# First k load on the ScalarE queue, contiguous turned rows, table transposes moved, and a new instruction plan, in a fused convolution and FFN kernel

## The chip, the cores and the metric

The kernel runs on one core of a Trainium2 chip. The metric is device time in microseconds (us) of one execution, the median of several runs. TensorE (PE in the profile) does the matmuls and transposes, VectorE (DVE) and ScalarE (ACT) the elementwise work and the copies out of PSUM, GpSimd (POOL) a few small operations, and SyncE (SP) issues most transfers. [...]

## The reference, cut to what matters

Two layers, each a gated long convolution (A) and a gated feed-forward network (B), on x of 2048 rows by 512 channels:

```python
def _A_ref(q, k, v, shift_k, ssm_k, ssm_D):
    k_shift = sum over t of k_pad[:, t:t+S, :] * shift_k[:, ks-1-t]     # 4 taps
    kv = k_shift * v
    y = irfft(rfft(kv padded to 2S) * rfft(ssm_k padded to 2S))[:S]     # long convolution over the rows
    return q * (y + kv * ssm_D)

def _B_ref(x, w_gate, w_up, w_down):                                    # D = 512, F = 1792
    return (silu(x @ w_gate) * (x @ w_up)) @ w_down

x = A_q
for layer in (0, 1):
    x = x + _A_ref(layernorm(x), A_k, A_v, A_shift_k, A_ssm_k, A_ssm_D)
    x = x + _B_ref(layernorm(x), B_w_gate, B_w_up, B_w_down)
```

(The loop and the sum over t are written out in the original; padding is shortened here.) The convolution result y does not depend on x or the layer, so it is computed once and used in both layers.

## The kernel before

The rows are cut into four blocks of 512, each held as 128 partitions by R = 4 rows. The long convolution is done block by block with cosine and sine tables ("fwd", and "inv", their transposes): each block of kv and of ssm_k (h) is turned into a spectrum by matmuls ("ps<-vt,fwd", "ps<-hs,fwd"), spectra are multiplied on VectorE ("t", "Z"), and matmuls with "inv" give y. The shift by taps is a matmul, too: four matmuls per 128 channels with diagonal matrices "dg" that hold the taps.

A planner in the kernel's own Python puts every operation into a list with an engine, an assumed cost and the buffers it reads and writes, and then fixes each engine's order by those costs. Where it foresees that TensorE is idle, it fills in matmuls on the identity ("wm"), whose results nobody reads:

```python
    def issue(self, seq, place, when, warm_until, warm):
        ...
                if start < warm_until and start - t > 0.5:
                    for ring, i in [(r, i) for r in ("pf", "pd", "pc") for i in range(self.rings[r])]:
                        if busy.get((ring, i), 0.0) <= t:
                            n = int((start - t - 0.4) / 0.085)
                            if n > 0:
                                warm(ring, i, n)
                            break
```

PSUM has eight buffers in three rings: "pf" (4), "pc" (2) and "pd" (2). The start of the program, for the first block:

```python
    def load_k(b, due=None, after=()):
        if b == 0:
            kn[b] = new("s8", "kn", [P, R, D])
            add("SP", 0.55, lambda: nc.sync.dma_start(out=kn[b].t[:], in_=k_t[:, b]), w=[kn[b]], lat=4.0, due=due)
            return
        ...                                   # other blocks: a transposing transfer

    def transpose_k(b, ring, engs):           # block 0: turned on TensorE, copied out by ACT and DVE in turn
        kT[b] = new("k", "kTb", [P, KD, PADL + L], parts=KD + 1)
        ...
        for dt in range(KD):
            pt = new(ring, "pt", [P, R, P], BF16)
            ...                               # four transposes of kn into pt (L379)
            dst = lambda dt=dt: kT[b].t[:, dt, PADL:PADL + L].rearrange("d (p r) -> d r p", r=R)
            ...                               # copy pt to dst (L383 ACT, L385 DVE)

    def shift_mul(b, ring, conv, after=()):
        for r in range(R):
            ...                               # per dt, per tap j:
                       [(kT[b].t[:, dt, PADL + r - j:PADL + r - j + R * (P - 1) + 1:R], dg.t[:, dt, j, :])
                        for j in range(KS)]
            ...                               # block 0: DVE multiplies the result by vt (L502)

    ...
    add("PE", 0.25, turn_taps, r=[tapR, ident], w=[pt4])                   # L928
    add("DVE", 0.1, lambda: nc.vector.tensor_copy(out=tapT.t[:], ...))     # L930
    for dt in range(KD):
        add("DVE", 0.6, ... out=dg.t[:, dt], ident * tapT[:, dt] ...)      # L933, four diagonals each
    transpose_k(0, "pf", ("ACT", "DVE"))
    hs = transpose_h(0, "pf", (2, 0, 1, 3), False, ("ACT", "DVE"))         # L475, L479, L482
    ...
    shift_mul(0, "pf", False)
    ...                                                                    # statistics, spectrum of h
    for n in range(2):
        it = new("pf", "it", [P, NI, P])
        ...                                   # seven transposes of fwd (L953), copied to inv by ACT (L955)
    X[0] = spectrum("X0")
    direct(vt[0], X[0], "pf", ("ACT", "ACT"))                              # spectrum of kv, block 0
    for slot in (0, 2, 1, 3):
        product(0, 0, [slot], False)                                       # L620, L624
```

The FFN of one unit (a layer, a block, and half of its rows) takes gate and up matmuls into "pf" (zT is the normalised x, turned), Silu and a copy on ScalarE (L837, L841), their product on VectorE (L844), and down matmuls into "pd" (L851). The result is added to x by VectorE (L870), or, in units that X_PE names, x is fed into the same PSUM sum by one more matmul (L817) for each 128 rows. Other switches choose engines unit by unit: ST1 and ST2 compute the sums of the layernorm on ScalarE, N_ACT and Z_ACT apply it there.

Of the kernel before, what the change touches and what calls it, by code (L numbers as in the profile page):

```python
# [9 lines left out]
P = 128  # L10
# [3 lines left out]
ACT = mybir.ActivationFunctionType  # L14
# [2 lines left out]
LN_EPS = 1e-5  # L17

NB = 4
SLK = 8.52  # L20
H_DMA = lambda b: b in {2, 3}
ST1 = lambda l, c, h: (l, c, h) in {(0, 1, 1), (0, 2, 0), (0, 3, 0), (1, 0, 1)}
ST2 = lambda l, c, h: (l, c, h) in {(0, 1, 1), (0, 3, 1), (1, 0, 0)}
ASL = 8.04
K_ACT = lambda b: b in {3}
PASSES = 1
PW = 1.2
PD_ACT, KV_ACT, ST_ACT = True, True, False
HSL = 13.4
Z_ACT = lambda l, c, h: (l, c, h) in {(0, 3, 1), (1, 1, 0), (1, 1, 1)}  # L30
N_ACT = lambda l, c, h: (l, c, h) in {(0, 2, 0), (0, 2, 1), (1, 2, 1), (1, 3, 0), (1, 3, 1)}
Z_DMA = lambda i, j: False
D_DMA = lambda l, c, h: False
X_PE = lambda l, c, h: (l, c, h) in {(0, 3, 1), (1, 1, 0), (1, 2, 0), (1, 3, 1)}
RINGS = {}
T0, FLOOR = 37.71, 9.21
DUR = [20.73, 19.38, 17.95, 16.46, 26.14, 17.1, 26.09, 16.75, 22.3, 20.61, 21.16, 19.35, 17.53, 22.2, 16.85, 27.0]
STRETCH = {1: {"PE": 2.88, "DVE": 1.23, "ACT": 4.33, "POOL": 1.0, "SP": 160.46},
           2: {"PE": 3.08, "DVE": 1.77, "ACT": 1.75, "POOL": 1.0, "SP": 1.07},
           3: {"PE": 3.04, "DVE": 1.08, "ACT": 2.72, "POOL": 1.0, "SP": 1.04}}  # L40
R = 4


# [23 lines left out]
class Plan:  # L67
# [1 line left out]

    LOOSE = ("pc", "ks")  # L70
    WAIT = {"PE": 0.1, "DVE": 0.15, "ACT": 0.1, "POOL": 0.1, "SP": 0.1}
    SAME = {"PE": 0.0, "DVE": 0.06, "ACT": 0.05, "POOL": 0.1, "SP": 0.0}
    CROSS = {"PE": 0.3, "DVE": 0.2, "ACT": 0.25, "POOL": 0.15, "SP": 0.0}

    def __init__(self, rings):
# [196 lines left out]
def kernel(  # L272
# [14 lines left out]
    nc = tc.nc  # L287
# [26 lines left out]
    def new(ring, name, shape, dtype=BF16, parts=1):  # L314
        space = psp if ring in ("pf", "pc", "pd") else pool

        def make(slot):
            tag = f"{ring}{slot}" if ring != "one" else name
            return space.tile(list(shape), dtype, name=name, tag=tag)
        return plan.buf(ring, name, make, parts)  # L320
# [35 lines left out]
    def load_h(b, eng="SP", due=None, after=()):  # L356
        hn[b] = new("s8" if b == 1 else "h", "hn", [P, KD, L], parts=1)
        q = nc.sync if eng == "SP" else nc.scalar
        return add(eng, 0.55, lambda: q.dma_start(out=hn[b].t[:], in_=h3[:, :, b * L:(b + 1) * L]), w=[hn[b]], lat=(5.0, 10.0)[b] if b < 2 else 6.0, due=due, after=after)

    def load_k(b, due=None, after=()):
        if b == 0:
            kn[b] = new("s8", "kn", [P, R, D])
            add("SP", 0.55, lambda: nc.sync.dma_start(out=kn[b].t[:], in_=k_t[:, b]), w=[kn[b]], lat=4.0, due=due)
            return
        kT[b] = new("s8" if b == 1 else "k", "kTb", [P, KD, PADL + L])
        add("SP", 2.2, lambda: nc.sync.dma_start_transpose(out=kT[b].t[:], in_=k3[b * L - PADL:(b + 1) * L]),
            w=[kT[b]], lat=12.0 if b == 1 else 8.0, due=due, after=after)

    def transpose_k(b, ring, engs):  # L370

        kT[b] = new("k", "kTb", [P, KD, PADL + L], parts=KD + 1)
        add("POOL", 0.2, lambda: nc.gpsimd.memset(kT[b].t[:, :, 0:PADL], 0.0), w=[(kT[b], (KD,))])
        for dt in range(KD):
            pt = new(ring, "pt", [P, R, P], BF16)

            def go(pt=pt, dt=dt):
                for r in range(R):
                    nc.tensor.transpose(pt.t[:, r, :], kn[b].t[:, r, dt * P:(dt + 1) * P], ident.t[:])  # L379
            add("PE", pe(R, P), go, r=[kn[b], ident], w=[pt])  # L380
            dst = lambda dt=dt: kT[b].t[:, dt, PADL:PADL + L].rearrange("d (p r) -> d r p", r=R)
            if engs[dt % len(engs)] == "ACT":
                add("ACT", act(D), lambda pt=pt, dst=dst: nc.scalar.copy(out=dst(), in_=pt.t[:]), r=[pt], w=[(kT[b], (dt,))])  # L383
            else:
                add("DVE", tt1(D), lambda pt=pt, dst=dst: nc.vector.tensor_copy(out=dst(), in_=pt.t[:]), r=[pt],  # L385
                    w=[(kT[b], (dt,))])

    def load_v(b, due=None, after=()):
# [172 lines left out]
    def transpose_h_dma(b):  # L561
        hr = new("s8", "hr", [P, R, KD, P], parts=KD)
        hs = new("hs", "hs", [P, R, D], parts=R)
        for dt in range(KD):
            add("ACT", act(D), lambda dt=dt: nc.scalar.copy(
                out=hr.t[:, :, dt], in_=hn[b].t[:, dt, :].rearrange("d (p r) -> d r p", r=R)), r=[hn[b]], w=[(hr, (dt,))],
                conv=True)
        for r in range(R):
            turned[b] = add("SP", 1.25, lambda r=r: nc.sync.dma_start_transpose(
                out=hs.t[:, r].rearrange("p (k f) -> p k f", k=KD), in_=hr.t[:, r]), r=[hr], w=[(hs, (r,))], lat=3.0 if b == 1 else 1.4, conv=True)  # L570
        return hs

    def shift_mul_t(b):

        a, c = new("s8", "ka", [P, 2, R, KD, P], parts=2 * KD), new("s8", "kc", [P, 2, R, KD, P], parts=2 * KD)
        for j, (t, h) in ((3, (a, 0)), (2, (a, 1)), (1, (c, 0)), (0, (c, 1))):
            for dt in range(KD):
                add("ACT", 0.615, lambda j=j, t=t, h=h, dt=dt: nc.scalar.activation(
                    out=t.t[:, h, :, dt], in_=kT[b].t[:, dt, PADL - j:PADL - j + L].rearrange("d (p r) -> d r p", r=R),
                    func=ACT.Copy, scale=tapF.t[:, dt, j:j + 1]), r=[kT[b], tapF], w=[(t, (h * KD + dt,))], conv=True)  # L580
        for t, h in ((a, 1), (c, 0), (c, 1)):
            dve(4 * D, lambda t=t, h=h: nc.vector.tensor_add(out=a.t[:, 0], in0=a.t[:, 0], in1=t.t[:, h]),
                [(t, range(h * KD, h * KD + KD))], [(a, range(KD))], conv=True)
        ks = c
        for r in range(R):
            add("SP", 1.25, lambda r=r: nc.sync.dma_start_transpose(
                out=ks.t[:, 0, r], in_=a.t[:, 0, r]), r=[(a, range(KD))], w=[(c, (r,))], lat=4.0, conv=True)
        for h in range(2):
            sl = slice(2 * h, 2 * h + 2)
            dve(2 * D, lambda sl=sl: nc.vector.tensor_mul(  # L590
                out=vt[b].t[:, sl, :], in0=ks.t[:, 0, sl].rearrange("p r k d -> p r (k d)"), in1=vt[b].t[:, sl, :]),
                [(c, (2 * h, 2 * h + 1))], [(vt[b], (2 * h, 2 * h + 1))], conv=True)
# [214 lines left out]
    def ffn(unit):  # L807
# [78 lines left out]
                                             allow_small_or_imprecise_dtypes=True), w=[fq], due=-50)  # L886
    add("POOL", 0.6, lambda: make_identity(nc, ident.t[:]), w=[ident])
    add("ACT", 1.5, lambda: nc.scalar.activation(out=warm1.t[:], in_=nhalf.t[:], func=ACT.Silu), r=[nhalf], w=[warm1], due=-50)
    load_k(0, -60)
    tapR = new("dn", "tapR", [KD, P, KS])  # L890
    add("SP", 0.5, lambda: nc.sync.dma_start(out=tapR.t[:], in_=A_shift_k.rearrange("(dt p) j -> dt p j", p=P)), w=[tapR],
        lat=2.4, due=-70)
    load_h(0, "ACT", -59)
    ph = new("s8", "ph", [P, NS, P], I32, parts=2)
    load_v(0, -59)
# [32 lines left out]
            nc.tensor.transpose(pt4.t[:, j, :], tapR.t[:, :, j], ident.t[0:KD, 0:KD])  # L928
    add("PE", 0.25, turn_taps, r=[tapR, ident], w=[pt4])
    add("DVE", 0.1, lambda: nc.vector.tensor_copy(out=tapT.t[:], in_=pt4.t[:].rearrange("p j dt -> p dt j")), r=[pt4], w=[tapT])  # L930
    add("DVE", 0.1, lambda: nc.vector.tensor_copy(out=tapF.t[:], in_=tapT.t[:]), r=[tapT], w=[tapF])
    for dt in range(KD):
        add("DVE", 0.6, lambda dt=dt: nc.vector.tensor_tensor(  # L933
            out=dg.t[:, dt], in0=ident.t[:].rearrange("p (o f) -> p o f", o=1).to_broadcast((P, KS, P)),
            in1=tapT.t[:, dt, :].rearrange("p (j o) -> p j o", o=1).to_broadcast((P, KS, P)), op=ALU.mult),
            r=[ident, tapT], w=[(dg, (dt,))])
# [9 lines left out]
        half(hs, ev, par, 2.0 / N, "pf", ("ACT", "ACT"), False)  # L946
        butterfly(ev, G[0], par, False)
    for n in range(2):
        it = new("pf", "it", [P, NI, P])

        def go(it=it, n=n):
            for i in range(NI):
                nc.tensor.transpose(it.t[:, i, :], fwd.t[:, n * NI + i, :], ident.t[:])  # L953
        add("PE", pe(NI, P), go, r=[fwd, ident], w=[it])
        add("ACT", act(NI * P), lambda it=it, n=n: nc.scalar.copy(out=inv.t[:, n * NI:(n + 1) * NI, :], in_=it.t[:]),  # L955
            r=[it], w=[(inv, (n,))])
# [64 lines left out]

    with tc.manual_schedule(engines={mybir.EngineType.DVE, mybir.EngineType.Activation, mybir.EngineType.PE,
                                     mybir.EngineType.Pool, mybir.EngineType.SP}):
        plan.issue(*plan.order(PASSES), T0, warm)

# [1 line left out]
_INS = ['A_q', 'A_k', 'A_v', 'A_shift_k', 'A_ssm_k', 'A_ssm_D', 'B_x', 'B_w_gate', 'B_w_up', 'B_w_down']  # L1027
# [26 lines left out]
```

## Time and profile before

| | |
|---|---|
| time, median of 3 runs | 357.86 us (357.56 to 357.94) |
| span of the profiled execution | 356.5 us |
| TensorE busy | 347.6 us |
| VectorE busy | 281.1 us |
| ScalarE busy | 238.0 us |
| GpSimd busy | 39.3 us |
| first matmul of the FFN starts | 37.09 us |

Busy time of an engine is the time in which it has an instruction at work; matmuls are pipelined, so the duration of one (0.38 us for 512 columns) is longer than the distance from one to the next. A line of the timeline gives the start, the length, the engine, the source line, the operation, the tiles it writes and reads, and how many instructions are merged; in brackets stands how long the engine was idle before it and who ended that. A line of the waits gives the total, the number and the longest in us. A row of the DMA list ends with the median time from issue to landing in us.

### The profile page before, as it was taken

Reading aid. Unit: us, or ns where it says so; the run is one execution under the profiler, and the core shown is the slowest. Engines: PE = TensorE matmul, PEld = TensorE weight load, DVE = VectorE, ACT = ScalarE, POOL = GpSimd, SP = SyncE. Lnnn points to the kernel's source line nnn. Section 1 sums busy time; section 2 is a strip of 40 time slices with the busy share of each in tenths; the row PEclk is TensorE's granted clock in tenths of the full one; section 3 lists DMA queues with packets and bytes.
Section 4 is the critical chain, followed back from the end, with each engine's and each line's share of the span. In section 5 each row is a group of like instructions: output and inputs, shape, how many; then the busy total and the mean of one; then the engine's idle time right before and its main releaser. Section 6 shows DMA issues by size and latency. Waiting matters only on the chain.

```text
span 356.5 us, 6735 instructions
## 1 busy us (share of the span) xinstructions
PE 347.6 (97%) x2689; PEld 254.4 (71%) x2712; DVE 281.1 (79%) x517; ACT 238.0 (67%) x454; POOL 39.3 (11%) x42
## 2 busy tenths in 40 slices
PE   7999999999999999999999999999999999999996
PEld 6655985867778585868668685858686777768673
DVE  6997999999989999999999999889985323626020
ACT  4587693838878493648878994848484775647352
POOL 1010010130320200111121000201101000101000
PEclk9999999999999999999999999999999999999999
DMA  7999021010241341010311042010103020101000
GB/s 263 306 353 293 2 69 22 0 31 2 45 119 45 63 147 31 0 31 1 79 40 31 1 116 63 2 29 3 31 29 31 30 31 1 31 1 31 30 2 29
DMA packets 37897, 21.98 MB, mean 62 GB/s; under 512 B 29797, under 2 KB 35690, under 8 KB 37866
## 3 DMA queue, kind: packets, MB, share of 16 engines
q1 hardware_dynamic: 37336, 21.03, 22.9%
q10 hardware_dynamic: 530, 0.53, 0.5%
q8 instruction: 21, 0.34, 0.4%
q14 instruction: 10, 0.08, 0.1%
HBM read 12.33 MB, written 2.10 MB: 40 GB/s over the span
## 4 chain that ended last, share of the span: by engine, by line
PE 49%; DVE 35%; ACT 10%; POOL 3%; issue 2%; DMA 1%; ACTq 0%; POOLq 0%; DVEq 0%
PE pf L335 30%; PE pd L851 15%; DVE m L518 4%; DVE ht L844 3%; DVE bnst L706 3%; DVE t L641 3%; DVE t L635 3%; DVE t L651 2%; POOL rstd L736 2%; ACT H L423 2%; DVE Z L656 2%; PE ps L335 2%; PE wm L1020 1%; DVE t L620 1%; DVE Z L648 1%
## 5 line engine op out<-in xcount | busy, mean ns | idle before, releaser
L335 PE MATMUL pf<-zT,wu_sb 128*128 128x256 bf16 x896 | 116.1, 273 | 0.1
L335 PE MATMUL pf<-zT,wg_sb 128*128 128x256 bf16 x896 | 116.1, 273 | 0.0
L335 PEld LDWEIGHTS <-wg_sb 128*128 128x128 bf16 x896 | 87.6, 98 | 18.9 <-issue 0.8
L851 PE MATMUL pd<-wd_sb,ht 128*128 128x512 bf16 x434 | 98.6, 380 | 1.5 <-DVE ht L844 0.8
L335 PEld LDWEIGHTS <-wu_sb 128*128 128x128 bf16 x896 | 87.6, 98 | 11.1
L837 ACT ACTIVATE sg<-pf 128x512 bf16<-128x512 f32 x112 | 68.9, 615 | 18.2 <-PE pf L335 16.7
L851 PEld LDWEIGHTS <-ht 128*128 128x128 bf16 x448 | 43.6, 98 | 49.8 <-DVE ht L844 1.2
L841 ACT CAST ht<-pf 128x512 bf16<-128x512 f32 x112 | 67.3, 601 | 15.0 <-PE pf L335 14.6
L844 DVE TENSOR_TENSOR ht<-ht,sg 128x1024 bf16<-128x1024 bf16 x64 | 39.5, 619 | 25.7 <-ACT ht L841 25.7
L711 POOL TENSOR_TENSOR rstd<-ve,nhalf 128x2 f32<-128x2 f32 x25 | 26.0, 1039 | 203.2 <-DVE ve L709 180.8
L706 DVE BATCH_NORM_STATS2 bnst<-xc 128x6 f32<-128x512 bf16 x50 | 32.5, 685 | 6.2 <-ACT xc L857 5.6
L863 ACT CAST dn<-pd 128x512 bf16<-128x512 f32 x24 | 12.9, 591 | 34.5 <-PE pd L851 34.5
L870 DVE TENSOR_TENSOR xc<-xc,dn 128x1024 bf16<-128x1024 bf16 x12 | 8.2, 686 | 17.8 <-ACT dn L863 17.8
L635 DVE TENSOR_TENSOR t<-X,G 128x2048 bf16<-128x2048 bf16 x18 | 21.9, 1219 | 0.0
L641 DVE TENSOR_TENSOR t<-X,G 128x2048 bf16<-128x2048 bf16 x18 | 21.9, 1217 | 0.0
L736 POOL TENSOR_TENSOR rstd<-ve,nhalf 128x2 f32<-128x2 f32 x7 | 12.0, 1719 | 80.0 <-DVE ve L732 80.0
L423 ACT ACTIVATE X<-ps 128x512 bf16<-128x512 f32 x32 | 18.8, 635 | 1.2 <-PE ps L335 1.1
L423 ACT ACTIVATE H<-ps 128x512 bf16<-128x512 f32 x24 | 13.4, 645 | 4.3 <-PE ps L335 4.3
L656 DVE TENSOR_TENSOR Z<-Z,t 128x2048 bf16<-128x2048 bf16 x12 | 14.7, 1222 | 0.1
L651 DVE TENSOR_TENSOR t<-t,t 128x2048 bf16<-128x2048 bf16 x12 | 14.6, 1221 | 0.1
L335 PE MATMUL ps<-vt,fwd 128*128 128x512 bf16 x54 | 14.4, 380 | 0.1
L335 PEld LDWEIGHTS <-fwd 128*128 128x128 bf16 x96 | 9.3, 98 | 7.2
(95 smaller groups left out, 316.5 us busy)
## 6 DMA issues: line engine op xcount, KB each, us to landing
vt<-in_A_v_dram SPq DMA_DIRECT2D x4, 512.0 KB, 4.6
xc<-in_A_q_dram SPq DMA_DIRECT2D x4, 512.0 KB, 4.8
out_dram<-xc SPq DMA_DIRECT2D x16, 128.0 KB, 1.7
wg_sb<-in_B_w_gate_dram SPq DMA_DIRECT2D x1, 1792.0 KB, 9.2
wu_sb<-in_B_w_up_dram SPq DMA_DIRECT2D x1, 1792.0 KB
wd_sb<-in_B_w_down_dram SPq DMA_DIRECT2D x1, 1792.0 KB, 12.3
hn<-in_A_ssm_k_dram SPq DMA_DIRECT2D x3, 512.0 KB, 7.6
hn<-in_A_ssm_k_dram ACTq DMA_DIRECT2D x1, 512.0 KB, 3.9
```

The source lines that it names most:

```text
L335: nc.tensor.matmul(o, lhsT=lhsT, rhs=rhs, start=(n == 0), stop=(n == len(terms) - 1))
L423: add("ACT", act(D), lambda: nc.scalar.activation(out=view(), in_=ps.t[:], func=ACT.Copy, scale=scale), r=[ps], w=[(buf, keys)], conv=conv)
L635: dve(n * D, lambda t1=t1, part=part: nc.vector.tensor_mul(out=t1.t[:], in0=x.t[:, sl, 0, :], in1=g.t[:, sl, part, :]), [(x, key(slots, (0 ...
L641: dve(n * D, lambda t2=t2, part=part: nc.vector.tensor_mul(out=t2.t[:], in0=x.t[:, sl, 1, :], in1=g.t[:, sl, 1 - part, :]), [(x, key(slots ...
L651: dve(n * D, lambda t1=t1, t2=t2, comb=comb: nc.vector.tensor_tensor(out=t1.t[:], in0=t1.t[:], in1=t2.t[:], op=comb), [t2], [t1], conv=conv)
L656: dve(n * D, lambda t1=t1, part=part: nc.vector.tensor_add(out=z.t[:, sl, part, :], in0=z.t[:, sl, part, :], in1=t1.t[:]), [t1], [zk], con ...
L706: add("DVE", 0.6, lambda st=st, i=i: nc.vector.bn_stats(out=st.t[:], in_=xs[c].t[:, i, :]), r=[(xs[c], (i,))], w=[st])
L711: add("POOL", PW, lambda: nc.gpsimd.tensor_tensor(out=rstd.t[:], in0=ve.t[:], in1=nhalf.t[:].to_broadcast((P, n)), op=ALU.pow), r=[ve, nha ...
L837: add("ACT", act(D), lambda ps=ps, o=o, sg=sg: nc.scalar.activation(out=sg.t[:, o:o + 2, :], in_=ps.t[:], func=ACT.Silu), r=[ps], w=[(sg, ...
L841: add("ACT", act(D), lambda ps=ps, o=o, ht=ht: nc.scalar.copy(out=ht.t[:, o:o + 2, :], in_=ps.t[:]), r=[ps], w=[(ht, (o // 2,))], due=(uni ...
L844: dve(n * W, lambda sg=sg, ht=ht: nc.vector.tensor_mul(out=ht.t[:], in0=ht.t[:], in1=sg.t[:]), [sg], [ht], due=(unit, k / pairs, 0.0, "h"))
L851: nc.tensor.matmul(pds[o].t[:], lhsT=ht.t[:, q, o * P:(o + 1) * P], rhs=wt["d"].t[:, ft, :], start=(ft == 0 and not xpe), stop=(ft == NF - 1))
```

## The change

The first block of k is loaded from ScalarE's queue ahead of h, and no longer from SyncE's. The turned k is stored contiguously: the copy now reads PSUM with a stride and writes one run, where it read one run and wrote with a stride. One of the four groups of tap diagonals is made on ScalarE by four scaled copies of the identity. The transposes of the table use the "pd" ring and may run earlier. The costs and latencies that the planner assumes are altered (among them the landing of the taps, 2.4 to 4.3 us), and so are its switches by unit and its other settings; with them every engine's order. It is meant to start the dense work of TensorE sooner and to spread the elementwise work better.

```diff
-SLK = 8.52
+SLK = 9.39
 ...                                      (ASL, HSL, T0, FLOOR, DUR, STRETCH: other settings of the planner)
-ST1 = lambda l, c, h: (l, c, h) in {(0, 1, 1), (0, 2, 0), (0, 3, 0), (1, 0, 1)}
-ST2 = lambda l, c, h: (l, c, h) in {(0, 1, 1), (0, 3, 1), (1, 0, 0)}
+ST1 = lambda l, c, h: (l, c, h) in {(0, 2, 0), (0, 3, 1), (1, 0, 1)}
+ST2 = lambda l, c, h: (l, c, h) in {(0, 1, 0), (0, 1, 1), (0, 3, 1), (1, 0, 0)}
-Z_ACT = lambda l, c, h: (l, c, h) in {(0, 3, 1), (1, 1, 0), (1, 1, 1)}
-N_ACT = lambda l, c, h: (l, c, h) in {(0, 2, 0), (0, 2, 1), (1, 2, 1), (1, 3, 0), (1, 3, 1)}
+Z_ACT = lambda l, c, h: (l, c, h) in {(0, 1, 1), (0, 3, 0), (0, 3, 1), (1, 0, 0), (1, 0, 1), (1, 1, 1), (1, 2, 0), (1, 2, 1), (1, 3, 1)}
+N_ACT = lambda l, c, h: (l, c, h) in {(0, 2, 1), (0, 3, 0), (0, 3, 1), (1, 1, 0), (1, 3, 0)}
-X_PE = lambda l, c, h: (l, c, h) in {(0, 3, 1), (1, 1, 0), (1, 2, 0), (1, 3, 1)}
+X_PE = lambda l, c, h: (l, c, h) in {(0, 2, 0), (0, 2, 1), (1, 3, 1)}
@@ load_k, block 0
-            add("SP", 0.55, lambda: nc.sync.dma_start(out=kn[b].t[:], in_=k_t[:, b]), w=[kn[b]], lat=4.0, due=due)
+            add("ACT", 0.5, lambda: nc.scalar.dma_start(out=kn[b].t[:], in_=k_t[:, b]), w=[kn[b]], lat=4.6, due=due)
@@ transpose_k
-            dst = lambda dt=dt: kT[b].t[:, dt, PADL:PADL + L].rearrange("d (p r) -> d r p", r=R)
+            dst = lambda dt=dt: kT[b].t[:, dt, PADL:PADL + L].rearrange("d (p r) -> d p r", r=R)
+            src = lambda pt=pt: pt.t[:].rearrange("d r p -> d p r")
...
@@ the start
-    load_k(0, -60)
+    load_k(0, -70)
     tapR = new("dn", "tapR", [KD, P, KS])
     add("SP", 0.5, lambda: nc.sync.dma_start(out=tapR.t[:], ...), w=[tapR],
-        lat=2.4, due=-70)
+        lat=4.3, due=-70)
...
-    add("DVE", 0.1, lambda: nc.vector.tensor_copy(out=tapF.t[:], in_=tapT.t[:]), r=[tapT], w=[tapF])
-    for dt in range(KD):
+    add("DVE", 0.1, lambda: nc.vector.tensor_copy(out=tapF.t[:], in_=pt4.t[:].rearrange("p j dt -> p dt j")), r=[pt4], w=[tapF])
+    for j in range(KS):
+        add("ACT", 0.32, lambda j=j: nc.scalar.activation(out=dg.t[:, KD - 1, j, :], in_=ident.t[:], func=ACT.Copy,
+                                                          scale=tapF.t[:, KD - 1, j:j + 1]), r=[ident, tapF], w=[(dg, (KD - 1,))])
+    for dt in range(KD - 1):
         add("DVE", 0.6, lambda dt=dt: nc.vector.tensor_tensor(
...
-        it = new("pf", "it", [P, NI, P])
+        it = new("pd", "it", [P, NI, P])
...
-        plan.issue(*plan.order(PASSES), T0, warm)
+        plan.issue(*plan.order(PASSES), 32.0, warm)
```

More of the change, by code (lines that the diff above doesn't have):

```diff
@@ L19 @@
 NB = 4
-SLK = 8.52
+SLK = 9.39
 H_DMA = lambda b: b in {2, 3}
-ST1 = lambda l, c, h: (l, c, h) in {(0, 1, 1), (0, 2, 0), (0, 3, 0), (1, 0, 1)}
-ST2 = lambda l, c, h: (l, c, h) in {(0, 1, 1), (0, 3, 1), (1, 0, 0)}
-ASL = 8.04
+ST1 = lambda l, c, h: (l, c, h) in {(0, 2, 0), (0, 3, 1), (1, 0, 1)}
+ST2 = lambda l, c, h: (l, c, h) in {(0, 1, 0), (0, 1, 1), (0, 3, 1), (1, 0, 0)}
+ASL = 4.93
 K_ACT = lambda b: b in {3}
@@ L28 @@
 PD_ACT, KV_ACT, ST_ACT = True, True, False
-HSL = 13.4
-Z_ACT = lambda l, c, h: (l, c, h) in {(0, 3, 1), (1, 1, 0), (1, 1, 1)}
-N_ACT = lambda l, c, h: (l, c, h) in {(0, 2, 0), (0, 2, 1), (1, 2, 1), (1, 3, 0), (1, 3, 1)}
+HSL = 8.56
+Z_ACT = lambda l, c, h: (l, c, h) in {(0, 1, 1), (0, 3, 0), (0, 3, 1), (1, 0, 0), (1, 0, 1), (1, 1, 1), (1, 2, 0), (1, 2, 1), (1, 3, 1)}
+N_ACT = lambda l, c, h: (l, c, h) in {(0, 2, 1), (0, 3, 0), (0, 3, 1), (1, 1, 0), (1, 3, 0)}
 Z_DMA = lambda i, j: False
 D_DMA = lambda l, c, h: False
-X_PE = lambda l, c, h: (l, c, h) in {(0, 3, 1), (1, 1, 0), (1, 2, 0), (1, 3, 1)}
+X_PE = lambda l, c, h: (l, c, h) in {(0, 2, 0), (0, 2, 1), (1, 3, 1)}
 RINGS = {}
[L36 to L40, printed above, removed]
+T0, FLOOR = -4.91, -25.25
+DUR = [25.78, 17.38, 27.0, 25.33, 24.61, 20.95, 21.66, 16.0, 20.19, 21.8, 21.11, 25.85, 19.67, 26.45, 17.91, 25.24]
+STRETCH = {1: {"PE": 5.28, "DVE": 1.49, "ACT": 3.3, "POOL": 1.0, "SP": 110.68},
+           2: {"PE": 1.3, "DVE": 1.9, "ACT": 1.37, "POOL": 1.0, "SP": 1.4},
+           3: {"PE": 2.03, "DVE": 1.56, "ACT": 1.6, "POOL": 1.0, "SP": 1.97}}
 R = 4
@@ L71 @@
     WAIT = {"PE": 0.1, "DVE": 0.15, "ACT": 0.1, "POOL": 0.1, "SP": 0.1}
-    SAME = {"PE": 0.0, "DVE": 0.06, "ACT": 0.05, "POOL": 0.1, "SP": 0.0}
+    SAME = {"PE": 0.0, "DVE": 0.12, "ACT": 0.05, "POOL": 0.1, "SP": 0.0}
     CROSS = {"PE": 0.3, "DVE": 0.2, "ACT": 0.25, "POOL": 0.15, "SP": 0.0}
@@ L358, in load_h @@
         q = nc.sync if eng == "SP" else nc.scalar
-        return add(eng, 0.55, lambda: q.dma_start(out=hn[b].t[:], in_=h3[:, :, b * L:(b + 1) * L]), w=[hn[b]], lat=(5.0, 10.0)[b] if b < 2 else 6.0, due=due, after=after)
+        return add(eng, 0.55, lambda: q.dma_start(out=hn[b].t[:], in_=h3[:, :, b * L:(b + 1) * L]), w=[hn[b]], lat=(5.5, 10.0)[b] if b < 2 else 6.0, due=due, after=after)
     def load_k(b, due=None, after=()):
@@ L380, in transpose_k @@
             add("PE", pe(R, P), go, r=[kn[b], ident], w=[pt])
-            dst = lambda dt=dt: kT[b].t[:, dt, PADL:PADL + L].rearrange("d (p r) -> d r p", r=R)
+            dst = lambda dt=dt: kT[b].t[:, dt, PADL:PADL + L].rearrange("d (p r) -> d p r", r=R)
+            src = lambda pt=pt: pt.t[:].rearrange("d r p -> d p r")
             if engs[dt % len(engs)] == "ACT":
-                add("ACT", act(D), lambda pt=pt, dst=dst: nc.scalar.copy(out=dst(), in_=pt.t[:]), r=[pt], w=[(kT[b], (dt,))])
+                add("ACT", 0.57, lambda src=src, dst=dst: nc.scalar.copy(out=dst(), in_=src()), r=[pt], w=[(kT[b], (dt,))])
             else:
-                add("DVE", tt1(D), lambda pt=pt, dst=dst: nc.vector.tensor_copy(out=dst(), in_=pt.t[:]), r=[pt],
+                add("DVE", tt1(D), lambda src=src, dst=dst: nc.vector.tensor_copy(out=dst(), in_=src()), r=[pt],
                     w=[(kT[b], (dt,))])
@@ L564, in transpose_h_dma @@
         for dt in range(KD):
-            add("ACT", act(D), lambda dt=dt: nc.scalar.copy(
+            add("ACT", 0.565, lambda dt=dt: nc.scalar.copy(
                 out=hr.t[:, :, dt], in_=hn[b].t[:, dt, :].rearrange("d (p r) -> d r p", r=R)), r=[hn[b]], w=[(hr, (dt,))],
@@ L577, in shift_mul_t @@
             for dt in range(KD):
-                add("ACT", 0.615, lambda j=j, t=t, h=h, dt=dt: nc.scalar.activation(
+                add("ACT", 0.66, lambda j=j, t=t, h=h, dt=dt: nc.scalar.activation(
                     out=t.t[:, h, :, dt], in_=kT[b].t[:, dt, PADL - j:PADL - j + L].rearrange("d (p r) -> d r p", r=R),
```

## The prediction

> **What bounds the kernel now.** I read the page's busy shares and slices first, then TensorE's waits, then the timeline of the first 40 us.
>
> ```profile
> PE 347.6 (97%) x2689; PEld 254.4 (71%) x2712; DVE 281.1 (79%) x517; ACT 238.0 (67%) x454; POOL 39.3 (11%) x42
> PE   7999999999999999999999999999999999999996
> PEclk9999999999999999999999999999999999999999
> ```
>
> TensorE (PE) is busy in every slice but the two ends, at the full granted clock. Its waits show how little there is to win back:
>
> ```profile
> PE wm L1020 <- POOL ident masks.py:199: 1.7, 1, 1.7
> PE pt L475 <- ACT kTb L383: 1.5, 2, 0.8
> PE pd L851 <- DVE ht L844: 0.8, 2, 0.6
> ```
>
> Three releasers, 4.0 us in all: 1.7 at the very start, 1.5 in the transposes of h, and only 0.8 in the 320 us after 37 us. So the span is the moment when TensorE's dense work begins, plus that work, plus a tail. The page's chain gives DVE 35%, but mostly where TensorE is just as busy beside it. The timeline of TensorE (start, length, operation) shows the beginning:
>
> ```profile
> 1.72 3.27 PE L1020 MATMUL wm<-ident 128*128 128x128 bf16 x29 [1.72 <-POOL ident masks.py:199]
> 5.05 0.26 PE L928 MATMUL pt<-ident,tapR 4*128 4x4 bf16 x4
> 5.25 1.77 PE L1020 MATMUL wm<-ident 128*128 128x128 bf16 x17
> 7.07 1.05 PE L379 MATMUL pt<-ident,kn 128*128 128x128 bf16 x16
> 8.85 0.39 PE L475 MATMUL pt<-ident,hn 128*128 128x128 bf16 x4 [0.73 <-ACT kTb L383]
> 9.99 0.94 PE L475 MATMUL pt<-ident,hn 128*128 128x128 bf16 x12 [0.76 <-ACT kTb L383]
> 10.77 3.74 PE L335 MATMUL ps<-dg,kTb 128*128 128x128 bf16 x64
> ...
> 17.80 0.94 PE L953 MATMUL it<-ident,fwd 128*128 128x128 bf16 x14
> ```
>
> Up to 7.07 "wm" is filler [...]; from 10.77 (call it S, the first shift matmul) nothing waits. The 14 transposes of the table ("it") sit inside the dense part. The fronts beside it, ScalarE (ACT) and VectorE (DVE):
>
> ```profile
> 7.49 2.45 ACT L383 COPY kTb<-pt 128x512 bf16<-128x512 bf16 x2 [3.06 <-PE pt L379]
> ```
> ```profile
> 5.63 2.50 DVE L933 TENSOR_TENSOR dg<-ident,tapT 128x512 bf16<-128x512 bf16 x4
> 8.05 2.44 DVE L385 COPY kTb<-pt 128x512 bf16<-128x512 bf16 x2
> ```
>
> Each turned-k copy takes 1.22 us, double or more of a plain 512-wide copy, and these copies release S. Last, the page's DMA list:
>
> ```profile
> hn<-in_A_ssm_k_dram ACTq DMA_DIRECT2D x1, 512.0 KB, 3.9
> kn<-in_A_k_dram SPq DMA_DIRECT2D x1, 512.0 KB, 4.7
> ```
>
> The k load is issued at 1.19 on SyncE (SP) and lands 4.7 later, at 5.89. Its transposes begin at 7.07, because 17 fillers queued ahead run until then. **The k load is not what the start waits for.**
>
> [...] k landed at 5.89, yet its transposes stood behind filler until 7.07. [...] in this trace the two places differ by 5.89 against 0.73 + 3.9 = 4.63. [...] Whether a copy that reads PSUM 256 bytes apart suffers, no row here shows. That is my main doubt.
>
> **The change part by part.**
>
> *k first on ScalarE's queue.* Landing 5.89 → about 4.6, h about 1.5 later than now. But the new order has 51 fillers ahead of the tap transposes, against 29 before them and 17 after. Filler is spaced 104 ns: 29 weight loads span 3.01 us, less the last one's 0.10, over 28 intervals. 51 × 0.104 = 5.3, from 1.72 to 7.0; after the short handover of before (0.2) taps run at about 7.2 and k's transposes at about 7.4. **That is 0.3 later than 7.07, not earlier**, and the taps are 2.1 later than 5.05. Gain of this part: none.
>
> *Contiguous turned rows.* Four copies at 1.22 become about 0.6 (estimate: 0.565 for a ScalarE copy that reads with a stride and writes contiguously, "hr", four in 2.24 us; VectorE's 512-wide PSUM products are spaced 0.60). Two per engine: 1.2 us shorter on each.
>
> *One diagonal on ScalarE, taps later.* VectorE formed diagonals during 5.63–8.13, before k needed it; now they cannot begin before the taps. VectorE after taps at 7.2: two small copies, to 7.8 (0.3 latency, 0.09, 0.28 wait, as at 5.05 → 5.63); one diagonal 0.6 → 8.4; two k copies → 9.6; two diagonals → 10.8. The last is needed only at the third group of four matmuls, 0.5 after S. ScalarE: first k copy at 7.4 + 0.42 = 7.8 → 8.4; three 128-wide scalings at about 0.3 → 9.3; k copy → 9.9; fourth → 10.2; first h copy (frees the buffer that S writes) → 10.7. So **S comes at about 10.7 against 10.77**: −0.1, uncertain by 0.5. The shorter copies are spent on paying for late taps and for the diagonals.
>
> *Table transposes into the gap.* The 14 go between k's and h's transposes, where TensorE waits anyway; their PSUM is now "pd", so h's buffers stay free. Dense part: **−0.94 us**. Can VectorE follow? Between the last shift product and the first spectrum product it loses two table negations, the tap cast and one statistics pair (0.08 + 0.34), and the second normalise pair moves into a later GpSimd wait (0.81). ScalarE copies the tables in its old 3.75 us idle before the spectra (−1.6 there). The product chain then ends about S + 17.3 (was 18.2: the last Z at 28.98), while TensorE needs its last piece at S + 17.6. The whole 0.94 should reach the first FFN matmul (37.09 → about 36.1).
>
> *Replan.* Counting matmuls in the two orders: 448 down, 896 + 896 gate and up, all convolution groups equal; residual adds on TensorE 8 → 6, at 0.214 each (28 down matmuls take 5.99): **−0.43**. VectorE gets one more 0.61 addition, but normalising moves to ScalarE: "z" from 3 to 9 half-blocks at two 0.33 each, −4. I summed VectorE's durations from the first "m<-H" (35.62) up to each gate product, and TensorE's from its first FFN matmul (37.09) to the down matmul that needs it. The thinnest lead in the old order is 1.3 us, in the second unit, precisely where the trace shows the 0.65 stall at 78.05; elsewhere no less than 1.6. In the new order the thinnest is 2.2, unchanged in the first unit, and 2.6 in the second. So that stall should go: **−0.6**; and some new stall of a like size may appear that such sums can't see: **+0.6**.
>
> Sum: 357.86 − 0.1 − 0.94 − 0.43 − 0.6 + 0.6 = **356.4 us**, 0.4% less.
>
> **The rivals.**
>
> *The copies stay slow.* If reading PSUM with a stride costs 1.2 us, VectorE's last diagonal ends at 12.0 and ScalarE's first h copy at 11.9, S slips 1.1 to 1.2, and the gain is eaten: 357.6. [...] Against: strided reads from SBUF cost 0.565. One in four.
>
> *The earlier k does matter.* If filler ran fast, at 55 ns like the k transposes (1.05 less a 0.22 tail, over 15), 51 of them would end by 4.6, k would start near 5, S near 8.5, and the time would be 354.2. Against: all 46 recorded fillers keep about 100 ns, the second batch too. One in ten.
>
> *The replan brings stalls.* The later h holds back the gate weights (a GpSimd copy waits for h) and the transfers behind them by about 1.5 us. DMA engines are busy until 36 us; but up-weights are needed only at 40 and v's second block at 43. If one such transfer, or VectorE in the first two units, ends last, it costs 1 to 3 us: 358 to 359. Leads in my sums are wider than before, so one in eight.
>
> **Range and chances.** The certain parts are 0.94 and 0.43; S moves ±0.5, stalls ±0.8, and the slow copy reaches up by 1.2. Eight in ten: 355.0 to 358.2. Two per cent are 7.2 us. The waits to win back are 4.0 us in all, so a gain of that size is nearly excluded (0.01); a loss needs stalls in many units (0.02).
>
> **What would show it.** In the changed profile: filler in one run to about 7.0, kn landing near 4.6 and its transposes not before 7.2; kTb copies near 0.6 each; S at 10.3 to 11.2; the 14 "it" transposes before S; first "pf" near 36.1; six "pd<-xc" matmuls; no wait of over 1 us after 37 us. I am wrong if S is outside 10.2 to 11.5, if kTb copies take over 1 us, or if "pf" or "pd" waits for VectorE or a transfer.

## The result and the profile after

The changed kernel takes 355.05 us (354.44 to 355.21, 4 runs) against 357.8 (357.56 to 357.94, 4 runs) on the same chip: a ratio of 0.9921, 95% interval 0.9904 to 0.9938. That is 2.75 us less; the prediction had 1.46 less. The span of the profiled execution falls from 356.5 to 353.4 us, which is 3.1 and not 2.75: the old kernel's profiled execution took 358.32 us, 0.5 more than its median.

The page's first lines and the waits of TensorE in the changed kernel:

```profile
span 353.4 us, 6784 instructions
PE 347.8 (98%) x2716; PEld 254.9 (72%) x2716; DVE 276.4 (78%) x511; ACT 249.6 (71%) x470; POOL 38.2 (11%) x42
...
PEclk9999999999999999999999999999999999999999
```
```profile
PE wm L1024 <- POOL ident masks.py:199: 1.7, 1, 1.7
PE pf L335 <- ACT sg L838: 0.2, 1, 0.2
```

Of the 4.0 us of listed waits before, 1.9 are left, and 1.7 of them are the wait for the identity at the very start. Here is TensorE's timeline at the start (start, length, operation), the changed kernel's:

```profile
1.72 5.40 PE L1024 MATMUL wm<-ident 128*128 128x128 bf16 x51 [1.72 <-POOL ident masks.py:199]
7.18 0.27 PE L929 MATMUL pt<-ident,tapR 4*128 4x4 bf16 x4
7.37 1.07 PE L379 MATMUL pt<-ident,kn 128*128 128x128 bf16 x16
8.28 0.55 PE L957 MATMUL it<-ident,fwd 128*128 128x128 bf16 x7
...
10.57 3.73 PE L335 MATMUL ps<-dg,kTb 128*128 128x128 bf16 x64
...
34.96 1.05 PE L335 MATMUL ps<-dg,kTb 128*128 128x128 bf16 x16
35.94 1.03 PE L335 MATMUL pf<-zT,wg_sb 128*128 128x256 bf16 x8
```

The filler ahead of the taps is one run to 7.12, k's transposes start at 7.37 (7.07 before), the shift matmuls at 10.57 (10.77), and the table's transposes now lie ahead of them. The first FFN matmul comes at 35.94 instead of 37.09. The copies of the turned k, on ScalarE and VectorE, and the DMA list:

```profile
7.81 0.59 ACT L384 COPY kTb<-pt 128x512 bf16<-128x512 bf16 x1 [2.96 <-PE pt L379]
```
```profile
8.46 1.28 DVE L386 COPY kTb<-pt 128x512 bf16<-128x512 bf16 x2
```
```profile
kn<-in_A_k_dram ACTq DMA_DIRECT2D x1, 512.0 KB, 3.5
hn<-in_A_ssm_k_dram ACTq DMA_DIRECT2D x1, 512.0 KB, 7.2
```

A copy that reads PSUM with a stride and writes contiguously takes about 0.6 us here, half of the old one (1.22). Plain copies of 512 columns, "hs<-pt", took 0.63 us on ScalarE and 0.43 on VectorE in the old kernel. k is issued at 0.73 and lands at 4.2; h is issued at 1.15 and lands only at 8.4, where it landed at 4.6 before.

**Where the time went.** I cut each profile at the first shift matmul of the second block (36.12 us before, 34.96 after). From there to the end it is 356.5 − 36.12 = 320.4 before and 353.4 − 34.96 = 318.4 after: 1.93 us less by the unrounded spans. Up to the cut the profiles differ by 1.16 us. But the part behind the cut repeats (320.4 in run 11 as well), so the 0.5 us by which the old kernel's profiled execution was long lie ahead of it. By the times, the start is worth about 2.75 − 1.93 = 0.8 us (an estimate), and what is said below to be saved before the cut, against 36.12, is up to 0.5 too much.

Of the 1.9 us behind the cut, two residual matmuls fewer explain 0.43. The other 1.5 are pauses of TensorE, and the distances between starts show them. The longest one of the old kernel, and the longest one of the changed kernel:

```profile
75.78 1.62 PE L335 MATMUL ps<-dg,kTb 128*128 128x128 bf16 x26
78.05 1.68 PE L851 MATMUL pd<-wd_sb,ht 128*128 128x512 bf16 x7 [0.65 <-DVE ht L844]
```
```profile
206.12 1.03 PE L852 MATMUL pd<-wd_sb,ht 128*128 128x512 bf16 x4
207.32 1.03 PE L335 MATMUL pf<-zT,wg_sb 128*128 128x256 bf16 x8 [0.17 <-ACT sg L838]
```

Shift matmuls are 0.056 us apart (64 in 3.57 us at the start), so 26 of them hold TensorE for 1.46 us. It was 78.05 − 75.78 = 2.27, a pause of 0.81 where the bracket says 0.65. In the same way four down matmuls, 0.216 apart, leave 0.34 where the bracket says 0.17. Other pauses have no bracket at all. Here is one, first before, then after:

```profile
187.61 0.86 PE L335 MATMUL ps<-hs,fwd 128*128 128x512 bf16 x2
188.31 1.03 PE L335 MATMUL pf<-zT,wg_sb 128*128 128x256 bf16 x8
```
```profile
186.34 0.59 PE L335 MATMUL ps<-hs,fwd 128*128 128x512 bf16 x2
186.78 1.04 PE L335 MATMUL pf<-zT,wg_sb 128*128 128x256 bf16 x8
```

The same two matmuls hold TensorE for 188.31 − 187.61 = 0.70 us before and for 0.44 after: 0.26 us of pause. Only starts show this; the lengths overlap.

Counted so behind the cut, the old kernel has some 2.0 us of pauses: 1.14 in the two waits that the view lists (0.81 here and 0.33 near 179 us; the view gives 0.8 for both), and 0.9 in seven pauses of 0.03 to 0.27 us that it does not list. The changed kernel has 0.4: the new wait near 207 us and one pause of 0.09 that both have.

### The profile page after: what moved, and what is told of

It is laid out like the page before. It is cut to its first block, busy times and chain, and to the rows that moved or that the text cites. A ratio compares the mean times of both kernels' runs of the same rounds, so it can differ in the third digit from the quotient of the medians.

```text
span 353.4 us, 6784 instructions
## 1 busy us (share of the span) xinstructions
PE 347.8 (98%) x2716; PEld 254.9 (72%) x2716; DVE 276.4 (78%) x511; ACT 249.6 (71%) x470; POOL 38.2 (11%) x42
## 4 chain that ended last, share of the span: by engine, by line
PE 65%; DVE 26%; ACT 4%; issue 2%; POOL 2%; ACTq 0%; DVEq 0%; POOLq 0%
PE pf L335 36%; PE pd L852 18%; PE ps L335 8%; DVE ht L845 3%; DVE bnst L707 3%; DVE m L519 2%; DVE t L636 2%; DVE t L652 2%; DVE t L642 2%; ACT H L424 2%; DVE Z L657 2%; PE wm L1024 2%; DVE G L556 1%; DVE xc L778 1%; POOL rstd L712 1%
## 5 line engine op out<-in xcount | busy, mean ns | idle before, releaser
L852 PE MATMUL pd<-wd_sb,ht 128*128 128x512 bf16 x448 | 103.1, 379 | 0.0
L838 ACT ACTIVATE sg<-pf 128x512 bf16<-128x512 f32 x112 | 67.5, 603 | 26.1 <-PE pf L335 25.9
L842 ACT CAST ht<-pf 128x512 bf16<-128x512 f32 x112 | 66.0, 590 | 18.7 <-PE pf L335 18.1
L712 POOL TENSOR_TENSOR rstd<-ve,nhalf 128x2 f32<-128x2 f32 x25 | 29.1, 1163 | 207.0 <-DVE ve L710 185.8
L864 ACT CAST dn<-pd 128x512 bf16<-128x512 f32 x26 | 13.9, 589 | 25.1 <-PE pd L852 25.1
L751 ACT ACTIVATE z<-xc,nmr,rstd 128x512 bf16<-128x512 bf16 x18 | 13.6, 807 | 2.7 <-DVE nmr L744 2.6
L737 POOL TENSOR_TENSOR rstd<-ve,nhalf 128x2 f32<-128x2 f32 x7 | 7.8, 1117 | 70.5 <-DVE ve L733 70.5
L335 PE MATMUL ps<-vt,fwd 128*128 128x512 bf16 x56 | 15.2, 379 | 0.0
```

The source lines that it names most:

```text
L335: nc.tensor.matmul(o, lhsT=lhsT, rhs=rhs, start=(n == 0), stop=(n == len(terms) - 1))
L712: add("POOL", PW, lambda: nc.gpsimd.tensor_tensor(out=rstd.t[:], in0=ve.t[:], in1=nhalf.t[:].to_broadcast((P, n)), op=ALU.pow), r=[ve, nha ...
L838: add("ACT", act(D), lambda ps=ps, o=o, sg=sg: nc.scalar.activation(out=sg.t[:, o:o + 2, :], in_=ps.t[:], func=ACT.Silu), r=[ps], w=[(sg, ...
L842: add("ACT", act(D), lambda ps=ps, o=o, ht=ht: nc.scalar.copy(out=ht.t[:, o:o + 2, :], in_=ps.t[:]), r=[ps], w=[(ht, (o // 2,))], due=(uni ...
L852: nc.tensor.matmul(pds[o].t[:], lhsT=ht.t[:, q, o * P:(o + 1) * P], rhs=wt["d"].t[:, ft, :], start=(ft == 0 and not xpe), stop=(ft == NF - 1))
```

## The experiments

Cut at the same place, all runs stand as follows ("shift" is the start of the first block's shift matmuls, "cut" that of the second block's; ratios are to the old kernel in the same job).

| run | time, us | ratio, 95% interval | shift | cut | span − cut |
|---|---|---|---|---|---|
| before | 357.8 | | 10.77 | 36.12 | 320.4 |
| changed | 355.05 | 0.9921 (0.9904 to 0.9938) | 10.57 | 34.96 | 318.4 |
| 1 start only | 357.05 | 0.9978 (0.9969 to 0.9988) | 10.65 | 35.25 | 320.0 |
| 2 replan only | 356.09 | 0.9959 (0.9944 to 0.9974) | 10.78 | 35.85 | 318.5 |
| 3 filler 30 | 354.31 | 0.9918 (0.9898 to 0.9938) | 9.73 | 34.00 | 318.4 |
| 4 strided copies | 356.01 | 0.9958 (0.9943 to 0.9973) | 11.34 | 35.70 | 318.5 |
| 5 k from SyncE | 355.28 | 0.9929 (0.9912 to 0.9945) | 10.50 | 34.88 | 318.4 |
| 6 the same, filler 30 | 353.27 | 0.9871 (0.9857 to 0.9886) | 8.77 | 33.04 | 318.5 |
| 7 tables late | 355.51 | 0.9936 (0.9921 to 0.9951) | 10.02 | 35.18 | 318.5 |
| 8 switches only | 359.04 | 1.0034 (1.0022 to 1.0046) | 10.80 | 36.12 | 321.1 |
| 9 settings only | 358.98 | 1.0037 (1.0023 to 1.0051) | 10.66 | 35.73 | 321.4 |
| 10 as 5, no filler | 355.3 | 0.9933 (0.9918 to 0.9948) | 10.32 | 34.69 | 318.9 |
| 11 before, filler 29 | 359.64 | 1.0057 (1.0037 to 1.0077) | 10.93 | 38.49 | 320.4 |
| 12 diagonals on VectorE | 356.4 | 0.9963 (0.9948 to 0.9977) | 11.76 | 36.56 | 318.4 |
| 13 old residual set | 355.2 | 0.9931 (0.9915 to 0.9948) | 10.64 | 35.02 | 318.6 |
| 14 old normalising sets | 355.1 | 0.9928 (0.9914 to 0.9943) | 10.07 | 34.45 | 318.8 |
| 15 old statistics sets | 357.45 | 1.0013 (0.9998 to 1.0028) | 10.80 | 35.17 | 322.8 |

The last column is the reading to keep: whatever was done to the start, the new plan needs 318.4 to 318.9 us after the cut, so the start and the rest add. (It is worked out from the page's rounded spans and good to 0.1 us.)

**The two halves (1, 2).** Run 1 is the changed kernel with the old switch sets and planner settings; run 2 the old kernel with the new ones:

```diff
 # run 1, on the changed kernel; run 2 is the reverse edit on the old one
-SLK = 9.39 ... ST1, ST2, Z_ACT, N_ACT, X_PE, ASL, HSL, T0, FLOOR, DUR, STRETCH, SAME, two ACT costs as after
+SLK = 8.52 ... the same as before
```

> The changed kernel's start (k ahead of h, contiguous turned rows, one diagonal group on ScalarE, table transposes in the gap) with the old switches and planner settings. Theory: the start and the replan are separate gains, so the first FFN matmul comes at 35.9 us, as in the changed kernel (37.1 before), and the rest after it keeps its old small waits: 356.6 us, 1.2 below before. Rival: the small waits after 37 us were only a matter of how the start and the FFN lie against each other, and go with the shift alone: about 355.1 us.

> The old start with the new switches and planner settings. Theory: first FFN matmul stays at 37.1 us; after it 0.43 us go with two residual matmuls and 1.5 us with small waits of TensorE: 355.9 us, and no wait of VectorE near 78 us. Rival: only the two matmuls and the one listed wait count, 0.43 + 0.65: 356.8 us.

Against the profile before, run 1 saves 0.9 us before the cut and 0.4 after; run 2 0.3 before and 1.9 after. Run 2 came out as the theory had it (356.09 for 355.9). Run 1's time falls by less than expected, 0.8 us by the ratio instead of 1.2; four of its ten executions took 356.16 to 356.62 us and six, with the profiled one, 357.00 to 357.49. Its first FFN matmul was expected at 35.9 and came at 38.99, because the old settings put all 64 shift matmuls of the second block ahead of it; the cut, at 35.25, is the place to compare. Its rival is refuted. Counted by starts behind the cut, run 2 keeps 0.4 us of pauses and run 1 1.4: the pauses go with the replan, not with the shift in time, apart from the wait near 77 us, of which run 1 keeps only 0.06.

**What holds the start (3, 5, 6, 10, 11).** Run 3 shortens the first filler run; run 5 moves only the issue of k:

```diff
 # run 3
-                            n = int((start - t - 0.4) / 0.085)
+                            n = min(30, int((start - t - 0.4) / 0.085))
 # run 5: k first on SyncE, h so first on ScalarE; the planner and all orders of compute as they were
-            add("ACT", 0.5, lambda: nc.scalar.dma_start(out=kn[b].t[:], in_=k_t[:, b]), ...)
+            add("ACT", 0.5, lambda: nc.sync.dma_start(out=kn[b].t[:], in_=k_t[:, b]), ...)
 # run 6: both; run 10: run 5 with min(0, ...); run 11, on the old kernel: filler only ahead of the taps (29)
```

> The changed kernel with its first run of filler matmuls cut from 51 to 30; nothing else moves. Theory: the filler holds back the start. Taps are turned near 5.2 us, k near 5.4 (it lands at 4.2); h lands at 8.4 and then sets the shift matmuls, which begin near 9.6 us, not 10.57: 354.1 us. Rival: with less filler TensorE's array stays slow for longer, and what is gained in waiting is lost in slow transposes: shift matmuls near 10.5, 355.0 us.

> The changed kernel with k issued from SyncE, first in its queue, and h so first on ScalarE's; every engine's compute order stays as it is. Theory: with 51 fillers the transposes of k begin at 7.2 to 7.4 us whatever the loads do, and h, landing near 5 us instead of 8.4, is not waited for either: shift matmuls at 10.57 as before the edit, 355.0 us. Rival: the place of k ahead of h is part of the gain, or h's late landing a part of the loss: a change of 0.5 us or more either way.

> As the last, with the first filler run cut from 51 to 30. Theory: with little filler the landing of h at 8.4 us was the next limit (shift matmuls at 9.73); with h first on its queue it lands near 5 us, then the copies and scalings on ScalarE set the start: shift matmuls near 8.8 us, 353.4 us. Rival: the slow array (107 ns a transpose until about 6.6 us) or the late taps hold it at 9.6 or more: 354.2 us.

Run 3's TensorE timeline:

```profile
5.35 1.89 PE L379 MATMUL pt<-ident,kn 128*128 128x128 bf16 x16
...
8.37 0.41 PE L476 MATMUL pt<-ident,hn 128*128 128x128 bf16 x4 [0.52 <-DMA hn<-in_A_ssm_k_dram]
```

With less filler k is turned at 5.35, slowly (16 in 1.89 us, not 1.07), and TensorE then waits for h, because h was put behind k. The shift starts 0.8 us earlier. The time falls by 0.7, but its interval overlaps the changed kernel's (three of four executions took 354.23 to 354.38 us, one 355.85); the profile carries this verdict. In run 5 k lands at 0.74 + 3.5 = 4.2, as in the changed kernel, and h at 0.73 + 4.8 = 5.5 instead of 8.4, and nothing moves that these runs resolve (355.28; shift 10.50): the long filler hid the harm to h. So k need not stand ahead of h on ScalarE's queue; first on SyncE's, it lands as early. Run 6 has the shorter filler and the early h, and the shift starts at 8.77, which was expected to 0.03 us:

```profile
8.77 3.73 PE L335 MATMUL ps<-dg,kTb 128*128 128x128 bf16 x64
```

At 353.27 us it beats both kernels, and its interval lies clear of the changed kernel's.

> k from SyncE, h first on ScalarE, and no filler ahead of the taps. Theory: the taps are still turned at their landing, about 5.1 us; without filler the array is slow (107 ns a transpose, shift matmuls and spectra at half speed) [...] which costs 1 to 2 us over the version with 30: 354.5 to 355.3 us. Rival: the array's pace hardly matters there, since copies on ScalarE and VectorE set the pace up to the shift: 353.3 to 353.6 us.

> The old kernel with only its second run of 17 fillers taken out (the first 29 stay). Theory: k lands at 5.9 us and its transposes waited for filler until 7.07; now they begin at 5.9 to 6.0, at half speed, and the shift matmuls come about 0.8 us earlier: 356.9 us. Rival: the copies of k or the slow array hold the start where it was: 357.7 us.

Without any filler (run 10) the shift slips to 10.32 and the time to 355.3: the theory held, and the filler is worth 2.0 us in run 6. The 16 transposes of k took 1.89 us and the last 12 of h 1.49 (1.55 and 0.83 in run 6); the shift matmuls, 3.85 against 3.73, and the spectrum of h, 3.62 in both, were not at half speed. Run 11 was a miss. Its TensorE timeline and the page's clock row:

```profile
5.93 1.07 PE L379 MATMUL pt<-ident,kn 128*128 128x128 bf16 x16 [0.60 <-DMA kn<-in_A_k_dram]
...
10.55 0.58 PE L475 MATMUL pt<-ident,hn 128*128 128x128 bf16 x4 [0.56 <-DVE kTb L385]
10.93 5.96 PE L335 MATMUL ps<-dg,kTb 128*128 128x128 bf16 x64
```
```profile
PEclk9699999999999999999999999999999999999999
```

k was turned 1.1 us earlier, as expected (and in 1.07 us, not at half speed), but the shift still began at 10.93: in the old kernel VectorE's diagonals and slow copies end no earlier (the bracket at 10.55; VectorE copies k from 8.06 on, 8.05 before). And in this profile TensorE waited four times (0.60, 0.72, 0.77 and 0.56 us, the first until 5.93 and the last until 10.55), the granted clock was 0.50 from 8.8 to 15.6 us, and 64 shift matmuls took 5.96 us instead of 3.74. What lowered the clock is not shown. The kernel became 1.95 us slower. The drop does not explain all of that: the profile is of the longest of four executions (360.69 us, mean clock 0.99), and the other three took 358.95 to 359.98 at a mean clock of 1.0. What held those is not shown. So the prediction's sentence that k's load is not what the start waits for holds, but its picture of filler as the one thing in the way was too simple for the old kernel.

**The copies, the tables, the diagonals (4, 7, 12).**

```diff
 # run 4: the old layout of the copy, the same order
-            dst = ... .rearrange("d (p r) -> d p r", r=R);  src = pt.t[:].rearrange("d r p -> d p r")
+            dst = ... .rearrange("d (p r) -> d r p", r=R);  src = pt.t[:]
 # run 7
-        it = new("pd", "it", [P, NI, P])
+        it = new("pf", "it", [P, NI, P])
 # run 12: no copies of ident on ScalarE
-    for dt in range(KD - 1):
+    for dt in range(KD):
```

> The changed kernel with the turned rows of k written with the old stride (same order of instructions, read side contiguous again). Theory: four copies take about 1.3 us instead of 0.6; two on each engine stand before the last diagonal and the first copy of h, so the shift matmuls begin near 11.8 us (10.57): 356.3 us. Rival: the landing of h at 8.4 us and the transposes behind it set the start, and the copies are hidden: 355.1 us.

> The changed kernel with the 14 table transposes back in the old ring, which puts them behind the spectrum of h again. Theory: shift matmuls stay near 10.6 us and everything after the transposes moves by their 0.94 us: first FFN matmul at 36.9, 356.0 us. Rival: TensorE would wait for VectorE's product chain there anyway, and less than half of it shows: 355.4 us or less.

> The changed kernel with all four groups of tap diagonals on VectorE again (planned anew). Theory: VectorE has 0.6 us more before the shift, ScalarE 1.3 us less; the last diagonal ends near 11.4 us but is needed only 0.7 us into the shift matmuls, which then begin or stall to the same effect as a start near 10.8: 355.3 us. Rival: the diagonals on ScalarE were worth their whole 0.6 us: 355.7 us.

In run 4 TensorE waits for the copies, and the shift comes 11.34 − 6.84 = 4.50 us after the taps instead of 3.39, at 1.0 us in time:

```profile
10.62 0.61 PE L476 MATMUL pt<-ident,hn 128*128 128x128 bf16 x8 [0.76 <-DVE kTb L386]
```

The contiguous rows are worth 1 us in this start. In run 7 the way from the shift to the first FFN matmul is 36.16 − 10.02 = 26.14 us instead of 25.37: the tables' place is worth 0.77 of the 0.94 predicted. The time shows only 0.46, with overlapping intervals, since in its profiled execution the taps were turned at 6.62 (see the last section); that run alone doesn't decide it. In run 12 the shift begins 4.35 us after the taps, 0.96 later than in the changed kernel, and waits for ScalarE's copy of h (0.34). It was expected to cost 0.3, or 0.6 by the rival, and costs 1.35. The diagonals were planned anew and other orders moved with them, so the figure is that of a plan without ScalarE's help, not of four scalings.

**Which part of the replan (8, 9, 13, 14, 15).** Run 8 puts the five new switch sets into the old kernel, run 9 the new settings without the sets. Runs 13 to 15 put one group of old sets back into the changed kernel.

> The old kernel with the five new switch sets by unit (statistics, normalising, residual adds), old start, old planner settings. Theory: the switches relieve VectorE, and with that go the small waits of TensorE after 37 us: 355.9 us, as with the whole replan (356.09). Rival: it is the planner's settings that place the operations better; the switches give only the two matmuls, 0.43 us: 357.2 us.

> The old kernel with the new planner settings (costs, stretches, slacks, durations), old start and old switch sets. The switches alone made it slower (359.04). Theory now: settings and switches work only as a pair, tuned together; the settings alone give less than half of the 1.5 us of the whole replan: 357.0 us or more. Rival: the settings carry all of it and the switches only cost: 355.9 us or less, below the whole replan's 356.09.

> The changed kernel with only the old set of residual adds on TensorE (eight matmuls instead of six), planned anew. Theory: two matmuls more, 0.43 us, and the small waits stay away: 355.5 us. Rival: the sets and settings hang together, and any one set back brings waits of 1 us or more: 356.5 us or more.

> The changed kernel with only the old sets for normalising (8 half-blocks on ScalarE instead of 14), planned anew; VectorE gets some 4 us more over the span. Theory: this relief of VectorE is what takes the small waits away, so they come back: 356.0 us or more. Rival: VectorE has room, and nothing changes: 355.1 us.

> The changed kernel with only the old sets for the layernorm sums (seven half-blocks on ScalarE in both, but other ones), planned anew. Theory: the load does not change, only where it lies, so the time stays: 355.1 us. Rival: where it lies is what the tuning found, and waits of 1 us or more come back: 356.0 us or more.

Neither part alone is good: both are 1.3 us slower than the old kernel, though the pair saves 1.5. For run 8 both of my expectations were wrong; for run 9 the theory held. The old residual set costs about 0.1 us behind the cut, and its time can't be told from the changed kernel's: the two matmuls save 0.43, but the changed kernel pauses for about 0.33 near 207 us (the wait for ScalarE shown above), and run 13 does not. The normalising sets, which relieve VectorE of 3.2 us (279.6 busy in run 14, 276.4 in the changed kernel), move nothing. The statistics sets do, against my expectation. The waits of run 9, then of run 15:

```profile
PE pf L335 <- DMA zT<-z: 1.5, 1, 1.5
```
```profile
PE pf L335 <- DMA zT<-z: 2.1, 1, 2.1
```

Both combine the new settings with the old statistics sets, and in both TensorE waits until about 143.7 us for a turned z. Run 15's profile is of one of the six longest of twenty executions (359.58 to 359.80 us): after that wait the granted clock was 0.50 from 143.9 to 147.3 us, so that its 322.8 holds an estimated 1.7 us of slower matmuls (half of 3.4). The other fourteen, 356.81 to 357.96, are all longer than any of the changed kernel (at most 355.21). The new settings go with the new statistics sets: without them z comes too late. Which setting lets the other small pauses go was not tried.

## Why the prediction was right or wrong

In its profile the start was right by its own steps: taps at 7.2 (7.18), k's transposes at 7.4 (7.37), ScalarE's scalings at 0.3 each (three in 0.98), shift at 10.7 (10.57), first FFN matmul near 36.1 (35.94), k's load without effect (landed at 4.2, it stood behind filler until 7.37), tables nearly worth their 0.94 (0.77 in run 7, and 0.95 between the two profiles: 37.09 − 10.77 less 35.94 − 10.57). In part this was luck. The prediction had all fillers some 104 ns apart; by starts they are 107 apart up to a change of pace and 56 after it, and the last ones of the old kernel already showed the 56. Where the change came earlier or later, the same 51 fillers put the taps anywhere from 6.62 to 7.41 us. And by the times, the start gained about 0.8 us where its terms sum to 1.04. The rival of slow PSUM reads, whose one in four was the author's estimate, is refuted by the 0.6 us copies, the rival of the earlier k by the wait behind the filler. The 1.5 us by which h was to land later were 3.7, hidden by the filler.

**The step that failed is the term for TensorE's waits after 37 us**, "−0.6" for the stall at 78 us and "+0.6" for new ones. The waits view lists 0.8 us there, and I took this for all there was to win. By the distances of starts there were 2.0: the stall at 78 was 0.81, a second wait near 179 us, which the prediction left out, was 0.33, and unlisted pauses made 0.9. The replan saved 1.9 of this and brought one new wait of 0.33 near 207 us, about 1.5 net; run 2, with the old start, shows the same gain behind the cut (320.4 − 318.5 = 1.9 with the two residual matmuls). With −1.5 in place of 0 the sum would read 357.86 − 0.1 − 0.94 − 0.43 − 1.5 = 354.9, against 355.05 measured. The summed leads of VectorE did point to the stall near 78, but they could not see pauses of 0.03 to 0.27 us, nor that the settings alone would have brought a wait of 1.5 us (run 9).

The −0.43 of the residual adds was right as a count and too large as a gain (run 13). The relief of VectorE, predicted as 4 us, was right in not being counted (run 14).

## What to carry to other kernels

Where an engine is listed as always busy, take the distance between starts against the work in between. A list of waits leaves out short pauses and can show the long ones too short: here it gave 0.8 us after 37 us, and the starts gave 2.0. Look at filler as at any other work in the queue: with too much, earlier transfers were hidden behind it (k landed at 4.2 us and was turned from 7.37 on), with too little the array was slow (k's transposes took 1.89 us without filler in run 10, 1.07 with 51), and the best of the three amounts tried with k and h both early, 30, ended at 5.1 us, just before the taps were there (5.2, the wait of run 10). And when sets and settings were tuned together, test them together: each half can be slower than either whole.

## What the runs showed of the hardware that was not expected

The filler's starts are 107 ns apart until 6.8 us in the changed kernel (6.7 in the old one) and 56 ns from there. The page's clock row shows full clock throughout, but the clock record in the trace begins only at 6.74 us (6.64), at the change of pace. The k transposes took 1.89 us in run 3 and 1.07 in the changed kernel. The change of pace did not come after a fixed time: from the first filler it took 5.0 us in the changed kernel, 2.9 in run 9 and 5.8 in run 3, and what sets it is not shown. So the same 51 fillers let the taps be turned at 6.62 us in run 7, 6.84 in run 4, 7.18 in the changed kernel and 7.41 in run 12. That moves the whole start by up to 0.8 us from one profiled execution to another, more than some of the parts measured here.
